# Another hand-searched step order for an attention-and-FFN kernel, up to its fifth chunk

## The chip, the cores and the metric

One core of one Trainium2 chip. The metric is the device time of one execution in microseconds (us). Engines are written as the profile writes them: PE (TensorE matmul), PEld (TensorE weight load, beside PE), DVE (VectorE), ACT (ScalarE), POOL (GpSimd), SP (SyncE, which here only issues DMAs; SPq is its sequencer).

## What is computed

A linear attention with a decaying state, and a squared-ReLU feed-forward network (FFN) on its output. Batch 4, 8 heads, 768 positions, head width 48, so 3072 tokens of width 384; the FFN is 2048 wide. All float32.

```python
for t in range(S):                                    # 768 positions
    kt, vt, rt, wt = (k[:, :, t], v[:, :, t], r[:, :, t], w[:, :, t])
    cur = np.einsum('bhd,bhe->bhde', u[None] * kt, vt)
    y[:, :, t] = np.einsum('bhd,bhde->bhe', rt, state + cur)
    state = wt[:, :, :, None] * state + np.einsum('bhd,bhe->bhde', kt, vt)
...
h = np.maximum(x @ w_in, 0.0)                         # x: y as 3072 x 384; w_in 384 x 2048
return (h * h @ w_out)                                # w_out 2048 x 384
```

## The kernel before

**Tiling.** The positions are cut into 6 chunks of 128; with 4 batches there are 24 attention units, "chunk c, batch b". The attention of a chunk makes x (the FFN's input, transposed); the FFN of the same chunk follows while the attention of the next chunk goes on between its steps. The FFN of a chunk runs over 16 blocks of 128 hidden columns. Every product is made of three matmuls, of a high and a low part of either factor. In chunk 1 and for the first blocks of chunk 0 a block is done in two halves, of two batches (256 columns of tokens) each; elsewhere all four batches together (512 columns). An FFN block has a position number x, counted in full blocks along the program: chunk 0 has x = 0 to 15 and so on. Its steps are:

- **hp at x** (L860): 9 matmuls into one of only two PSUM tiles `hp0`, `hp1`.
- **g1** (ACT, L865): ReLU into a tile t. **g2** (ACT L867 in chunk 0, DVE L869 after): the square, back into hp. **g3** (ACT, L871): the high part g. **g4** (DVE, L872): the low part, hp minus g. Only after g4 is the hp tile free again.
- **ob at x** (L878): 3 matmuls for each batch into its output tile `ob`. They need both parts of g, so g4 too.

**Attention steps that the prediction names.** On DVE: z0, z1 (L480, transposes of loaded rows of a pair of batches), scan (L535, four running sums a unit), rt, kn, kn2, kq (L552, L558, L559, L562, whole-tile products), S (L697, L812) and S2 (L700), mask (L709), xl (L614). On ACT: far, far2 (L604, L605), Ec (L557), exp (L543), ly (L801), rc2 (L521). On POOL from chunk 2 on: rk and ru (L584, L586). On PE: turn (L518), ktp (L635) and mix (L668 to L687 are one group for a unit). On SP: load (L471), v (L504), pt (L490) and the sends (L725), which copy pieces of x between partitions.

**Splitting the weights.** Each of 16 weight tiles is widened on ACT (L428), treated in three DVE steps (L432, L436, L441), rounded on ACT (L448) and its rest formed on POOL (L449).

**Order.** The kernel records 2446 steps in a `Plan` and then emits them by three tables of numbers: `ORDER` holds the step numbers in the order of emission, `PLACES` says which buffer of its pool each tile gets, and `FILLS` puts so many dummy 128x128 transposes (L351) on PE ahead of a step. Each engine works through its own steps in that order and waits, in order, for what a step needs.

```python
order, places, fills = self.table or (range(len(self.steps)), (), {})
...
for n in order:
    s = self.steps[n]
    assert all(d.n in done for d in s.deps), ("too early", n, s.name)
    ...
    place = pool[places[self.slots[k]]] if places else next(...)
    ...
    if n in fills:
        s.fill = fills[n]
```

Of the kernel before, what the change touches and what calls it, by code (L numbers as in the profile page):

```python
# [96 lines left out]
class Names:  # L97
# [18 lines left out]
    4, 14, 17, 19, 6, 16, 0, 5, 20, 1, 18, 26, 15, 11, 7, 23, 24, 25, 55, 58, 309, 21, 22, 27, 28, 8, 2, 13, 30, 9, 57, 31, 312, 59, 33, 56, 64, 10, 29, 61,  # L116
    32, 92, 12, 36, 60, 308, 65, 53, 93, 62, 67, 38, 52, 71, 37, 310, 39, 51, 66, 63, 72, 3, 68, 311, 40, 102, 69, 106, 70, 74, 94, 105, 41, 73, 103, 107, 75,
    77, 108, 43, 42, 44, 46, 54, 45, 47, 48, 76, 314, 327, 78, 95, 104, 79, 49, 315, 109, 50, 313, 80, 81, 96, 111, 316, 317, 112, 34, 35, 82, 143, 318, 113,
    326, 146, 83, 346, 329, 97, 330, 118, 328, 84, 319, 85, 86, 320, 149, 87, 88, 89, 114, 110, 119, 180, 148, 345, 344, 147, 321, 150, 347, 90, 322, 115,
    323, 459, 116, 460, 348, 466, 91, 461, 462, 100, 101, 467, 99, 98, 184, 145, 468, 142, 324, 117, 144, 152, 463, 331, 469, 190, 470, 153, 155, 332, 181,  # L120
    333, 198, 139, 325, 124, 334, 140, 159, 141, 121, 151, 126, 464, 154, 120, 465, 472, 335, 349, 122, 125, 160, 350, 127, 182, 161, 351, 352, 156, 183, 353,
    128, 223, 336, 195, 162, 224, 129, 131, 185, 196, 337, 130, 471, 133, 132, 217, 473, 197, 157, 365, 338, 135, 134, 136, 474, 363, 158, 339, 382, 475, 137,
    138, 340, 480, 354, 476, 481, 482, 355, 483, 477, 165, 166, 364, 163, 362, 191, 192, 356, 167, 366, 168, 484, 341, 342, 169, 357, 487, 385, 384, 214, 216,
    358, 359, 488, 494, 489, 490, 491, 123, 360, 170, 193, 383, 343, 479, 194, 478, 172, 171, 361, 173, 380, 175, 210, 225, 174, 486, 201, 226, 493, 495, 176,
    202, 485, 233, 281, 496, 381, 497, 367, 498, 177, 368, 501, 164, 239, 199, 492, 502, 240, 503, 504, 500, 508, 392, 369, 370, 509, 510, 221, 511, 371, 505,
    372, 515, 499, 516, 393, 398, 507, 394, 512, 506, 517, 395, 222, 513, 227, 518, 519, 373, 396, 211, 230, 188, 514, 229, 397, 246, 386, 228, 522, 523, 387,
    529, 520, 521, 524, 525, 526, 388, 207, 400, 401, 200, 419, 530, 248, 231, 402, 234, 531, 532, 374, 533, 208, 527, 375, 528, 232, 251, 242, 536, 537, 389,
    538, 539, 203, 204, 543, 390, 249, 540, 376, 399, 544, 178, 220, 403, 420, 243, 437, 189, 535, 377, 534, 545, 546, 547, 215, 250, 247, 205, 391, 378, 179,
    438, 404, 405, 406, 552, 553, 554, 542, 555, 218, 379, 556, 561, 410, 407, 541, 562, 551, 563, 206, 564, 416, 565, 548, 550, 187, 557, 256, 408, 276, 262,
    261, 209, 264, 560, 549, 263, 411, 412, 413, 235, 570, 212, 219, 418, 236, 559, 213, 569, 571, 414, 284, 292, 186, 283, 291, 290, 558, 289, 417, 439, 409,  # L130
    265, 452, 572, 573, 574, 568, 579, 436, 237, 422, 241, 259, 423, 567, 576, 580, 566, 260, 581, 238, 424, 458, 425, 578, 582, 280, 244, 426, 415, 245, 304,
    435, 453, 427, 575, 583, 421, 428, 457, 454, 456, 455, 257, 287, 434, 641, 258, 285, 253, 266, 429, 297, 430, 431, 288, 440, 709, 441, 286, 432, 267, 442,
    277, 295, 588, 589, 577, 269, 597, 590, 586, 584, 707, 268, 433, 708, 591, 305, 598, 599, 600, 592, 643, 270, 644, 587, 254, 446, 642, 301, 652, 595, 255,
    271, 443, 585, 302, 601, 273, 272, 447, 594, 650, 606, 448, 303, 444, 445, 649, 648, 654, 647, 274, 658, 656, 653, 278, 655, 660, 593, 602, 646, 607, 659,
    608, 603, 279, 710, 645, 740, 275, 711, 596, 651, 252, 657, 609, 449, 296, 293, 294, 298, 615, 661, 718, 610, 664, 282, 1007, 616, 604, 667, 612, 673,
    611, 617, 670, 618, 741, 1022, 713, 722, 605, 668, 715, 669, 675, 676, 674, 624, 684, 1023, 1024, 299, 671, 723, 450, 677, 686, 625, 614, 613, 680, 619,
    300, 626, 672, 683, 451, 621, 678, 663, 665, 622, 306, 627, 681, 685, 307, 623, 679, 682, 666, 620, 628, 687, 742, 635, 743, 744, 695, 698, 632, 775, 776,
    714, 717, 745, 777, 638, 694, 720, 782, 629, 700, 778, 783, 712, 724, 779, 719, 789, 1025, 630, 633, 690, 784, 780, 781, 701, 705, 697, 785, 786, 726,
    790, 704, 796, 721, 716, 634, 788, 693, 791, 792, 797, 732, 793, 787, 794, 746, 689, 1014, 798, 696, 799, 730, 1026, 1012, 800, 631, 731, 803, 729, 688,
    736, 810, 699, 795, 692, 802, 804, 1008, 1013, 1051, 805, 801, 1011, 806, 702, 807, 811, 812, 813, 814, 817, 1010, 703, 733, 818, 735, 734, 819, 820, 809,  # L140
    691, 737, 1053, 808, 706, 816, 824, 821, 1027, 725, 815, 1018, 738, 739, 1028, 822, 825, 826, 1009, 827, 831, 832, 828, 747, 823, 830, 1052, 748, 1017,
    1055, 728, 833, 834, 1054, 1015, 727, 749, 760, 758, 835, 1066, 755, 764, 756, 838, 839, 840, 845, 829, 837, 836, 841, 842, 846, 1068, 847, 1062, 1058,
    1065, 852, 848, 849, 1016, 757, 763, 761, 853, 854, 844, 762, 636, 1057, 859, 843, 855, 1059, 765, 851, 1061, 1063, 856, 1134, 1135, 1136, 1137, 860, 861,
    862, 1084, 1064, 850, 866, 857, 1019, 858, 1020, 639, 867, 1067, 1060, 863, 771, 868, 1021, 869, 865, 870, 873, 880, 1056, 767, 773, 1138, 1073, 874,
    1085, 770, 864, 871, 1076, 875, 772, 662, 876, 1075, 881, 872, 774, 769, 877, 878, 882, 879, 1074, 1123, 1139, 883, 752, 1080, 1029, 884, 759, 768, 891,
    754, 1069, 885, 1071, 1164, 751, 753, 1077, 1030, 766, 1078, 1086, 1087, 898, 892, 893, 894, 1124, 1079, 899, 637, 1081, 1031, 1088, 1039, 895, 1082,
    1083, 1040, 888, 750, 905, 889, 900, 901, 902, 1034, 1163, 1165, 896, 1038, 1037, 1046, 912, 640, 906, 1140, 1089, 897, 907, 1126, 908, 1044, 913, 1119,
    904, 1070, 1120, 1041, 1045, 909, 1090, 1033, 1091, 1048, 914, 911, 1092, 1050, 903, 1049, 1043, 1036, 1125, 1072, 919, 1035, 915, 1042, 1166, 1047, 1093,
    916, 926, 1032, 1167, 1121, 920, 921, 1104, 1122, 1196, 1127, 1103, 1128, 1101, 922, 1180, 1096, 1178, 1179, 1177, 910, 917, 1197, 1100, 1106, 1102, 1169,
    927, 1098, 923, 1108, 933, 1198, 1095, 1099, 1112, 1105, 928, 929, 1107, 1199, 1130, 1170, 918, 925, 930, 1174, 934, 924, 1398, 1399, 935, 936, 1097, 940,  # L150
    931, 937, 941, 942, 1110, 947, 1094, 1109, 1129, 932, 939, 943, 944, 1168, 1176, 954, 1200, 938, 1173, 1175, 1171, 1172, 948, 1115, 1181, 1131, 1132, 945,
# [867 lines left out]
```

## Time and profile before

| | |
|---|---|
| runs | 522.84, 522.40, 522.19 us; median 522.4 us |
| profiled execution, its time | 521.4 us |
| its span | 519.7 us |
| granted TensorE clock | 1.00 |
| PE busy | 506.6 us, 97% |
| PEld busy | 458.5 us, 88% |
| DVE busy | 358.3 us, 69% |
| ACT busy | 319.1 us, 61% |
| POOL busy | 87.8 us, 17% |
| DMA | 48.74 MB, mean 94 GB/s |

The span is the time between the first and the last recorded instruction; the execution's own time lies 1.7 us above it. Busy shares are means over the whole program: DVE and ACT are full in the first 54 us, where the weights are split, and far from full at the end. Idle time stands in the rows below in brackets, with the instruction that ended it.

### The profile page before, as it was taken

Reading aid. Unit: us, or ns where it says so; the run is one execution under the profiler, and the core shown is the slowest. Engines: PE = TensorE matmul, PEld = TensorE weight load, DVE = VectorE, ACT = ScalarE, POOL = GpSimd, SP = SyncE. Lnnn points to the kernel's source line nnn. Section 1 sums busy time; section 2 is a strip of 40 time slices with the busy share of each in tenths; the row PEclk is TensorE's granted clock in tenths of the full one; section 3 lists DMA queues with packets and bytes.
Section 4 is the critical chain, followed back from the end, with each engine's and each line's share of the span. In section 5 each row is a group of like instructions: output and inputs, shape, how many; then the busy total and the mean of one; then the engine's idle time right before and its main releaser. Section 6 shows DMA issues by size and latency. Waiting matters only on the chain.

```text
span 519.7 us, 13752 instructions
## 1 busy us (share of the span) xinstructions
PE 506.6 (97%) x5452; PEld 458.5 (88%) x5452; DVE 358.3 (69%) x787; ACT 319.1 (61%) x878; POOL 87.8 (17%) x133
## 2 busy tenths in 40 slices
PE   8999999999999999999998999999999999999996
PEld 7888898888999998899987989889988888998895
DVE  6999789898687988768778658678476354333332
ACT  4999898996766867666573656564543363433232
POOL 3025233344021040212203001303000000000000
PEclk9999999999999999999999999999999999999999
DMA  7999977363847765575772480661181000100001
GB/s 152 225 165 247 246 151 205 88 92 63 148 71 100 147 97 95 106 125 73 117 129 37 84 137 15 112 122 36 32 133 32 3 19 6 59 16 0 1 2 65
DMA packets 188310, 48.74 MB, mean 94 GB/s; under 512 B 178000, under 2 KB 183120, under 8 KB 188240
## 3 DMA queue, kind: packets, MB, share of 16 engines
q1 hardware_dynamic: 187520, 46.82, 47.6%
q8 instruction: 45, 0.74, 0.6%
q10 hardware_dynamic: 720, 0.98, 0.5%
q14 instruction: 25, 0.20, 0.1%
HBM read 31.65 MB, written 4.72 MB: 70 GB/s over the span
## 4 chain that ended last, share of the span: by engine, by line
PE 78%; SPq 5%; issue 5%; DVE 4%; ACT 4%; DMA 2%; POOL 1%; POOLq 0%; ACTq 0%; DVEq 0%
PE ob L878 35%; PE hp L860 34%; PE ob L668 2%; SPq L504 2%; PE ob L687 2%; DMA ri<-in_moe_w_in_dram 2%; PE a L677 2%; SPq L415 1%; PE a L650 1%; PE hp L635 1%; SPq L471 1%; POOL wi L449 1%; DVE pt L535 1%; ACT t L865 1%; DVE m L550 1%
## 5 line engine op out<-in xcount | busy, mean ns | idle before, releaser
L878 PE MATMUL ob<-wo,g 128*128 128x384 f32 x1152 | 227.0, 340 | 0.1
L860 PE MATMUL hp<-x,wi 128*128 128x512 f32 (+1 forms) x1062 | 221.8, 355 | 3.2 <-DVE g L872 2.5
L878 PEld LDWEIGHTS ob<-wo,g 128*128 128x128 f32 x1152 | 199.4, 188 | 8.1 <-DVE g L872 0.9
L860 PEld LDWEIGHTS hp<-x,wi 128*128 128x128 f32 x1062 | 174.1, 188 | 29.7 <-DVE g L872 3.7
L869 DVE SCALAR_TENSOR_TENSOR hp<-hp,t 128x512 f32<-128x512 f32 (+1 forms) x96 | 58.2, 606 | 74.5 <-ACT t L865 74.2
L865 ACT ACTIVATE t<-hp 128x512 f32<-128x512 f32 (+1 forms) x118 | 61.0, 517 | 72.2 <-PE hp L860 47.7
L872 DVE TENSOR_TENSOR g<-hp,g 128x512 fp32r<-128x512 f32 (+1 forms) x118 | 69.1, 587 | 35.5 <-ACT g L871 35.0
L871 ACT CAST g<-hp 128x512 fp32r<-128x512 f32 (+1 forms) x118 | 59.6, 506 | 49.5 <-DVE hp L869 48.6
L630 ACT ACTIVATE m<-diag,beta 128x64 f32<-128x64 f32 x160 | 40.4, 338 | 3.4 <-DVE beta L593 3.3
L658 POOL MEMSET S<- 1x1 f32 x20 | 2.2, 110 | 237.4 <-PE ob L668 237.4
L614 DVE SCALAR_TENSOR_TENSOR x<-ob,x 112x128 fp32r<-112x128 f32 x80 | 21.2, 284 | 19.3 <-ACT x L611 16.5
L822 ACT COPY ob<-zero 112x128 f32<-112x128 f32 x80 | 20.7, 270 | 17.3 <-PE ob L878 10.1
L611 ACT ACTIVATE x<-ob 112x128 fp32r<-112x128 f32 x80 | 19.1, 275 | 17.3 <-PE ob L687 12.1
L535 DVE TENSOR_TENSOR_SCAN pt<-pt,zero 112x128 f32<-112x128 f32 x64 | 27.2, 456 | 2.4 <-DMA x<-x 1.1
L449 POOL TENSOR_TENSOR wi<-q,wi 128x768 fp32r<-128x768 f32 x8 | 17.1, 2135 | 55.1 <-ACT wi L448 44.0
L584 POOL TENSOR_TENSOR st<-st 128x384 f32<-128x384 f32 x16 | 16.7, 1043 | 33.0 <-DVE st L480 32.5
L480 DVE STREAM_TRANSPOSE st<-st 128x1152 f32<-128x1152 f32 x16 | 21.6, 1363 | 0.0
L542 ACT ACTIVATE m<-pt 112x512 f32<-112x512 f32 x24 | 15.1, 631 | 9.2 <-DVE pt L535 8.2
L449 POOL TENSOR_TENSOR wo<-q,wo 128x768 fp32r<-128x768 f32 x8 | 15.9, 1983 | 18.1 <-ACT wo L448 14.8
L558 DVE TENSOR_TENSOR pt<-pt,m 112x512 f32<-112x512 f32 x24 | 16.9, 706 | 2.4 <-ACT Ec L557 1.3
L559 DVE SCALAR_TENSOR_TENSOR m<-pt,m 112x512 f32<-112x512 f32 x24 | 18.0, 748 | 0.3
L709 DVE COPY_PREDICATED m<-caus,a 128x256 f32<-128x256 uint8 x40 | 17.3, 439 | 0.9 <-PE a L650 0.9
(125 smaller groups left out, 540.0 us busy)
## 6 DMA issues: line engine op xcount, KB each, us to landing
pt<-st SPq DMA_DIRECT2D x96, 96.0 KB, 2.9
ro<-in_moe_w_out_dram SPq DMA_DIRECT2D x8, 768.0 KB, 6.1
v<-in_v_dram SPq DMA_DIRECT2D x96, 48.0 KB, 2.8
out_dram<-q SPq DMA_DIRECT2D x20, 192.0 KB, 2.1
ri<-in_moe_w_in_dram SPq DMA_DIRECT2D x32, 96.0 KB, 4.9
ri<-in_moe_w_in_dram SPq DMA_DIRECT2D x8, 384.0 KB, 6.1
st<-in_r_dram SPq DMA_DIRECT2D x8, 384.0 KB, 5.3
st<-in_w_dram SPq DMA_DIRECT2D x8, 384.0 KB, 4.9
```

Of the source, the lines that this page charges most:

```text
L449: P.add("pool", 1.9, rank(8 * k + 5), lambda q=q, tt=tt: G.tensor_tensor(out=tt[:, 1], in0=q.tile, in1=tt[:, 0].bitcast(F32), op=ALU.subtr ...
L480: V.transpose(out=zt[:, i].rearrange("a t p q i -> a t (p q) i"), in_=sv[:, :, i].rearrange("s t p q x -> s t (p q) x"))
L535: lambda p=p: V.tensor_tensor_scan(out=pt[:, 0, p], data0=src(0)[:, p], data1=zero.broadcast_to([HP, C]), initial=1.0, op0=ALU.mult, op1=A ...
L614: made.append(P.add("dve", c2, rank(nm + "l"), lambda y=y, hi=hi, lo=lo: V.scalar_tensor_tensor(out=lo(), in0=y(), scalar=-1.0, in1=hi().b ...
L630: A.activation(M.tile[:, o:o + Q], diag2, AF.Copy, scale=beta.tile[:, i:i + 1])
L822: P.add("act", 0.16, rank("zero"), lambda p=p: A.copy(out=obs[p][0:HP, DM:], in_=zero[0:HP].broadcast_to([HP, C])), w=[("YO", p)], after=t ...
L860: T.matmul(hp.tile[:, 0:n], wi[f][:, wl, kt], xT[:, kt, xl, xs], start=(m == 0), stop=(m == 3 * KT - 1))
L865: P.add("act", 0.49 if full else 0.28, rank("g1"), lambda: A.activation(t(), h(), AF.Relu), r=[hp], w=[(g, 1)])
L869: P.add("dve", 0.605 if full else 0.337, rank("g2"), lambda: V.scalar_tensor_tensor(out=h(), in0=h(), scalar=0.0, in1=t(), op0=ALU.max, op ...
L871: P.add("act", 0.48 if full else 0.26, rank("g3"), lambda: A.copy(out=hi(), in_=h()), r=[hp], w=[(g, 0)])
L872: P.add("dve", 0.605 if full else 0.335, rank("g4"), lambda: V.tensor_tensor(out=lo(), in0=h(), in1=hi().bitcast(F32), op=ALU.subtract), r ...
L878: T.matmul(obs[b][:, 0:DM], g.tile[0][:, gl, o:o + C], wo[f][:, wl], start=(f == 0 and m == 0), stop=(f == NF - 1 and m == 2))
```

## The change

Only the three tables differ. Every step, its instructions and its shapes are the same. From `zero of chunk 4, batch 0`, the 1739th of the 2446 steps, to the end the two orders are equal; before it nearly every engine's order differs in places. `FILLS` has 59 dummy transposes in place of 52.

```diff
 ORDER = (
-    4, 14, 17, 19, 6, 16, 0, 5, 20, 1, 18, 26, 15, 11, 7, 23, 24, 25, 55, 58, 309, 21, 22, 27, 28, 8, 2, 13, 30, 9, 57, 31, 312, 59, 33, 56, 64, 10, 29, 61,
...
 FILLS = {
-    16: (2, 'ob', 1), 55: (6, 'ob', 3), 30: (3, 'ob', 1), 57: (4, 'ob', 1), 71: (2, 'ob', 0), 48: (5, 'ob', 1), 82: (3, 'ob', 3), 89: (5, 'ob', 1),
-    145: (3, 'ob', 0), 144: (7, 'ob', 0), 127: (8, 'side', 0), 168: (4, 'side', 0),
+    16: (2, 'ob', 1), 15: (3, 'ob', 2), 57: (3, 'ob', 1), 55: (3, 'ob', 1), 71: (2, 'ob', 1), 41: (4, 'ob', 1), 77: (2, 'ob', 1), 80: (5, 'ob', 3),
+    143: (2, 'ob', 3), 459: (10, 'ob', 1), 145: (3, 'ob', 0), 144: (7, 'ob', 0), 127: (8, 'side', 0), 223: (3, 'side', 0), 473: (2, 'side', 0),
 }
```

What the tables do is seen in the order of the instructions. Three places follow; names end in a buffer number, and a row's last entry is its shape.

**DVE, around 74 to 79 us, the splits of weights 3 and 4 and the attention of chunk 1.** The last row is g4 at 12, the first full block (512 columns), which frees the tile for hp at 16. Before:

```order
L872 TENSOR_TENSOR g1_97<-hp0_151,g1_97 128x256
L432 TENSOR_SCALAR q1_156<-q1_156 128x768
L441 SCALAR_TENSOR_TENSOR q0_155<-ri4_72,q0_155 128x768
L558 TENSOR_TENSOR pt0_135<-pt0_135,m2_164 112x512
L872 TENSOR_TENSOR g2_99<-hp0_151,g2_99 128x256
L436 SCALAR_TENSOR_TENSOR q1_156<-ro3_70,q1_156 128x768
L812 TENSOR_TENSOR S3_140<-a1_154,Ec3_172 112x96
L441 SCALAR_TENSOR_TENSOR q1_156<-ro3_70,q1_156 128x768
L872 TENSOR_TENSOR g0_95<-hp1_152,g0_95 128x512
```

The same stretch of the changed kernel:

```order
L872 TENSOR_TENSOR g1_97<-hp1_152,g1_97 128x256
L432 TENSOR_SCALAR q1_156<-q1_156 128x768
L441 SCALAR_TENSOR_TENSOR q0_155<-ri4_72,q0_155 128x768
L436 SCALAR_TENSOR_TENSOR q1_156<-ro3_70,q1_156 128x768
L872 TENSOR_TENSOR g2_99<-hp0_151,g2_99 128x256
L441 SCALAR_TENSOR_TENSOR q1_156<-ro3_70,q1_156 128x768
L552 TENSOR_TENSOR pt0_135<-pt0_135 112x4x127
L558 TENSOR_TENSOR pt0_135<-pt0_135,m3_165 112x512
L559 SCALAR_TENSOR_TENSOR m3_165<-pt0_135,m3_165 112x512
L872 TENSOR_TENSOR g0_95<-hp1_152,g0_95 128x512
```

L436 of weight 3 (q1) now follows directly on L441 of weight 4 (q0); rt, kn and kn2 (L552, L558, L559) stand between L441 of weight 3 and g4.

**DVE, around 276 to 282 us, where chunk 4's attention begins.** L480 are z0 and z1 of batches 2 and 3, L535 the scans of batch 1, and the first L872 of each piece is g4 at 88. Before:

```order
L535 SCALAR_TENSOR_TENSOR pt0_135<-pt0_135,zero_126 112x128
L614 SCALAR_TENSOR_TENSOR x1_141<-ob2_149,x1_141 112x128
L480 STREAM_TRANSPOSE st0_157<-st1_158 128x1152
L869 SCALAR_TENSOR_TENSOR hp1_152<-hp1_152,t0_96 128x512
L480 STREAM_TRANSPOSE st0_157<-st1_158 128x1152
L535 SCALAR_TENSOR_TENSOR pt0_135<-pt0_135,zero_126 112x128 x3
L872 TENSOR_TENSOR g0_95<-hp1_152,g0_95 128x512
```

The same stretch of the changed kernel:

```order
L535 SCALAR_TENSOR_TENSOR pt0_135<-pt0_135,zero_126 112x128
L480 STREAM_TRANSPOSE st0_157<-st1_158 128x1152 x2
L614 SCALAR_TENSOR_TENSOR x1_141<-ob2_149,x1_141 112x128
L872 TENSOR_TENSOR g0_95<-hp1_152,g0_95 128x512
L697 TENSOR_TENSOR S10_173<-a0_153,S0_137 112x96
L535 SCALAR_TENSOR_TENSOR pt0_135<-pt0_135,zero_126 112x128
```

Three scans between z1 and g4 at 88 are moved behind it: one soon after, the other two after g4 at 92 and after g2 at 94. On PE, the first step that needs g4 at 88 was hp at 92, right behind hp at 90; now three ob at 88 stand between the two.

**SP, around 208 to 216 us, where chunk 2's x is completed.** L725 are the sends of its last batch; L889 is a store of an output. Before:

```order
L504 DMA v2_161<-in_v_dram 64x4x48 x2
L471 DMA st1_158<-in_w_dram 128x16x48
L889 DMA out_0_dram<-q1_156 128x384
L504 DMA v0_159<-in_v_dram 64x4x48
L725 DMA x0_142<-x3_168 16x2x256 x6
```

The changed kernel:

```order
L504 DMA v2_161<-in_v_dram 64x4x48
L504 DMA v0_159<-in_v_dram 64x4x48 x2
L471 DMA st1_158<-in_r_dram 128x16x48
L725 DMA x0_142<-x3_168 16x2x256 x6
L504 DMA v0_159<-in_v_dram 64x4x48
```

The six sends move ahead of that store, of a load (`in_w_dram`) and of a v.

## Rows read from the trace of the kernel before

**Rows 1.** The page: busy times of the engines, and the chain that ended last.

```profile
PE 506.6 (97%) x5452; PEld 458.5 (88%) x5452; DVE 358.3 (69%) x787; ACT 319.1 (61%) x878; POOL 87.8 (17%) x133
PE 78%; SPq 5%; issue 5%; DVE 4%; ACT 4%; DMA 2%; POOL 1%; POOLq 0%; ACTq 0%; DVEq 0%
```

**Rows 2.** Busy times by window: stretch, length, busy time (instructions), PEclk, DMA share, GB/s.

```profile
16.00:54.00 38.00, 35.50 (x515) 31.42 (x512) 35.43 (x67) 34.56 (x95) 11.05 (x6) 1.00 0.94 213
54.00:300.00 246.00, 242.82 (x2910) 222.25 (x2909) 199.25 (x444) 178.73 (x515) 59.47 (x76) 1.00 0.62 113
300.00:515.00 215.00, 214.67 (x1906) 192.72 (x1904) 112.18 (x235) 97.47 (x245) 13.15 (x31) 1.00 0.24 45
```

**Rows 3.** The waits of PE: what waited for what, total, times, longest.

```profile
PE hp L860 <- DVE g L872: 2.5, 2, 1.5
PE hp L518 <- DVE g L872: 0.9, 1, 0.9
```

**Rows 4.** Timeline near 50 us: start, length, engine and instruction, idle before it.

```profile
48.84 0.84 ACT L448 CAST wo<-q 128x768 fp32r<-128x768 f32 x1
49.46 0.96 DVE L436 SCALAR_TENSOR_TENSOR q<-ro,q 128x768 uint32<-128x768 uint32 x1
...
49.75 2.36 POOL L449 TENSOR_TENSOR wo<-q,wo 128x768 fp32r<-128x768 f32 x1 [2.11 <-ACT wo L448]
...
50.46 2.47 DVE L441 SCALAR_TENSOR_TENSOR q<-ro,q 128x768 uint32<-128x768 uint32 x1
...
53.31 0.65 PE L518 MATMUL hp<-ident,st 128*112 128x128 f32 x4 [0.87 <-DVE g L872]
```

**Rows 5.** Timeline from 74 to 80 us.

```profile
74.00 0.69 DVE L558 TENSOR_TENSOR pt<-pt,m 112x512 f32<-112x512 f32 x1 [1.29 <-ACT Ec L557]
...
74.78 1.84 POOL L449 TENSOR_TENSOR wi<-q,wi 128x768 fp32r<-128x768 f32 x1 [6.75 <-ACT wi L448]
74.94 2.49 DVE L436 SCALAR_TENSOR_TENSOR q<-ro,q 128x768 uint32<-128x768 uint32 x1
...
79.13 1.44 PE L860 MATMUL hp<-x,wi 128*128 128x512 f32 x5 [0.96 <-DVE g L872]
```

**Rows 6.** Timeline from 276 to 282 us.

```profile
277.85 1.00 POOL L584 TENSOR_TENSOR st<-st 128x384 f32<-128x384 f32 x1
277.88 3.42 DVE L535 TENSOR_TENSOR_SCAN pt<-pt,zero 112x128 f32<-112x128 f32 x3
278.05 2.37 PE L860 MATMUL hp<-x,wi 128*128 128x512 f32 x9
...
281.22 0.66 DVE L872 TENSOR_TENSOR g<-hp,g 128x512 fp32r<-128x512 f32 x1
...
281.94 2.36 PE L860 MATMUL hp<-x,wi 128*128 128x512 f32 x9 [1.52 <-DVE g L872]
```

**Rows 7.** Two lines of DVE over the whole program: minimum, median, maximum ns.

```profile
L441 DVE SCALAR_TENSOR_TENSOR q<-ro,q x8: 943/954/2468, 29.4 to 117.0; 128x768 uint32<-128x768 uint32 x8
...
L535 DVE TENSOR_TENSOR_SCAN pt<-pt,zero x64: 398/414/1251, 137.5 to 401.5; 112x128 f32<-112x128 f32 x64
```

**Rows 8.** Timeline around 200 us.

```profile
199.66 1.71 PEld L878 LDWEIGHTS ob<-wo,g 128*128 128x128 f32 x10 [0.38 <-DVE g L872]
...
201.96 0.60 PE L635 MATMUL hp<-ident,pt 112*128 112x112 f32 x4 [0.27 <-DVE pt L562]
```

**Rows 9.** Timeline from 208 to 217 us.

```profile
208.63 1.64 SPq L889 DMA_DIRECT2D out_dram<-q  x1
...
211.03 4.27 SPq L725 DMA_DIRECT2D x<-x  x6
...
214.53 2.63 DVE L480 STREAM_TRANSPOSE st<-st 128x1152 f32<-128x1152 f32 x2
...
216.82 3.52 PE L860 MATMUL hp<-x,wi 128*128 128x512 f32 x14 [0.31 <-DMA x<-x]
```

**Rows 10.** Timeline near 31 us: the fills in front of a waiting step.

```profile
31.66 0.93 PE L351 MATMUL ob<-ident 128*128 128x128 f32 x7
```

201 rows, old and new, of tables (ORDER, PLACES) are left out of this document.

## Prediction

> **What bounds the kernel now.** The page comes first. PE is busy 506.6 of 519.7 us and holds 78% of the chain that ended last [rows 1]; the clock is 1.00 all through, so it costs nothing that an order could give back. An order can only remove waits of PE, so the next view is busy time by window [rows 2]. From 300 us on, the part whose order stays, PE is idle 215.00 - 214.67 = 0.33 us. From 54 to 300 us it is idle 246.00 - 242.82 = 3.18 us, and from 16 to 54 us 38.00 - 35.50 = 2.50 us. In that second stretch PE is not the pace: DVE (35.43 of 38) and ACT (34.56) are nearly gapless and the DMA share is 0.94, while PE's own gaps are partly stuffed with dummy transposes, which count as busy: seven of them take 0.93 us, 0.13 each [rows 10].
>
> So what the change can remove as visible idle time is 2.50 + 3.18 = 5.7 us. The waits list says where most of it lies: three waits, 2.5 + 0.9 = 3.4 us, are all for a g4 [rows 3]. The timelines then show why each g4 was late, and it is one pattern three times. A DVE step with two operands in SBUF runs beside a POOL step and takes far longer than elsewhere: L441 2.47 us beside a POOL L449 [rows 4], with 0.954 as its median [rows 7]; L436 2.49 beside an L449 [rows 5]; three scans in 3.42 beside L584 [rows 6], with 0.414 each as the median [rows 7]. In each case the DVE step ends when the POOL step does, plus its own normal length: L449 ends at 49.75 + 2.36 = 52.11, L441 at 52.93. The g4 queued right behind it is late, and PE, which needs the hp tile that g4 frees, waits 0.87, 0.96 and 1.52 us.
>
> **The change, part by part.** No instruction of work is added or removed, so PE's work costs the same; seven fills more cost 7 x 0.13 = 0.9 us at the very most, and nothing where they stand in a wait. All else is a question of which wait goes and which comes.
>
> *The scans at 278 us.* Before, hp at 92 stands directly behind hp at 90 on PE, so g4 at 88 has only the 2.37 us of hp at 90 as cover, and it stands behind three held scans (3.42 us) [rows 6]. After, these scans stand behind g4, and on PE three ob at 88, which need g4 too, stand between hp at 90 and hp at 92; g4 loses 3.42 us of predecessors against a wait of 1.52. The two scans held back to g4 at 92 and g2 at 94 then meet the POOL steps, or miss them, with nothing of PE right behind. I take the whole wait: **-1.5** (bounds 0 and -1.5). What is late next is rt of that unit, and with it its mix, which PE needs only several FFN blocks later.
>
> *hp at 16, 79 us.* L436 of weight 3 now follows on L441 of weight 4 without kn and a half-size g4 between, so it is issued about a microsecond sooner and should start before the POOL step that held it; also the 1.29 us in which DVE waited for Ec [rows 5] goes, as kn is behind the splits. Against that rt, kn and kn2, some 0.69 each [rows 5], now stand ahead of g4 at 12, and two of these were not there before. Removed 2.49 - 0.95 = 1.5 and 1.3, added 2 x 0.69 = 1.4, and the following L441 may be held by the same L449 for up to its 1.84 us. The net, 1.4 without the last and -0.4 with it, is on average about half of the wait of 0.96: **-0.5** (bounds -1.0 and +0.4).
>
> *The first half of the FFN, 50 us.* On ACT the L448 that lets POOL start (48.84, 0.84 us [rows 4]) stands behind two more ACT steps after the change (rc2, a whole-tile step, for which I put the 0.69 of one [rows 5], and ly, a small one; together 0.9, an estimate), so L449 would start near 50.6 in place of 49.75; L441 would start at 50.46 plus whatever DVE is late by then (one step of xl and some scans are moved ahead, which I put at a quarter to one microsecond). If L441 starts first it takes 0.95 and the wait of 0.87 is gone; if L449 does, L441 ends at 50.6 + 1.84 + 0.95 = 53.4, half a microsecond later than the 52.93 of before. These two are nearly even. I take **-0.3** (bounds -0.9 and +0.6).
>
> *The waits near 200 us.* PEld waits 0.38 for a g4 and PE 0.27 for kq [rows 8]. More ob steps stand between hp and the first of them afterwards; I take that one whole and nothing of the other: **-0.4** (bounds 0 and -0.65).
>
> *The sends of chunk 2.* They are issued from 211.03 to 215.30, and hp at 64 waits 0.31 for the last to land [rows 9]. After the change they stand in front of a store whose issue took 1.64 us and of a load and a v, so the last lands earlier by more than 0.31: **-0.3** (bounds 0 and -0.3). Loads and v of a later chunk go that much later; a v is needed by mix, many blocks on.
>
> *New waits.* The moves also shorten covers. In front of g4 at 40, z1 and z0 now stand back to back, 2.63 us for two as in [rows 9], where one z and a mask stood, while what PE has between hp at 40 and hp at 42 gets no longer; in front of g4 at 78 a rt of 0.69 is put; z1 of chunk 4's first pair stands behind a later load. Each of these has little or no slack, and each costs nothing if DVE comes there with none of its work late. The nearest rows for one that fails are the three waits of before, 0.87 to 1.52. I take one of 0.9 and 0.1 for fills: **+1.0** (bounds 0 and +3.0, two or three failing at once).
>
> [...] The row shows L441 ending 0.82 us behind the L449 beside it [rows 4], about its own normal length: nothing of it went on meanwhile. [...]
>
> *Sum:* -1.5 - 0.5 - 0.3 - 0.4 - 0.3 + 1.0 = **-2.0 us**. The profiled execution took 521.4, so it would take 519.4. It lies 1.0 below the median of the runs, 522.4; moved by the same, the median of the changed kernel is **520.4 us**. Its own range, from one new wait more to none and the even case at 50 us won, is 519.0 to 521.6.
>
> **The rivals.**
>
> *More goes than named.* No new wait, the L441 at 50 us free, and the head of the FFN quicker because PE's stuffed gaps before 54 us shrink too: 520.4 - 1.0 - 0.6 - about 1 (less than the 2.50 idle in that window [rows 2]) gives 517.8. For it: DVE and ACT are so full up to 54 us that a better order there counts in full. Against it: the DMA share of 0.94 in the same stretch, which no order lowers.
>
> *The waits only change place.* POOL's 59.47 us between 54 and 300 us and DVE's 199.25 [rows 2] are the same steps; they must meet somewhere as often as before. The new places at x = 40 and 78 and at 50 us cost what the old ones did: 522.4, within 1.0. For it: the old order hid all but three or four meetings as well. Against it: at 278 us PE gets cover that it did not have, whatever POOL does.
>
> *Slower.* VectorE steps are held by POOL just ahead of a g4 in new places. At 1.1 us each (the mean of 0.87, 0.96 and 1.52), with the 1.5 at 278 us gained, it decides from the third such wait on: four give -1.5 - 0.7 + 4 x 1.1 = +2.2, or 524.6. For it: covers at 40 and 78 are short, and the even case at 50 us. Against it: many half-block covers of chunk 1 grew.
>
> **How the numbers follow.** The sum's own case 0.46; more goes 0.13; waits change place 0.23; slower 0.18. A measurement of this kernel can tell about 0.2%, 1.0 us. Faster by more (under 521.4): 0.13 of more goes and 0.44 of the sum's own, 0.57. Within: 0.21 of the places changed and 0.02 of the sum's own, 0.23. Slower: 0.18 and 0.02, 0.20. The range of 517.4 to 523.6 leaves out about 0.04 below and 0.14 above.
>
> **What would show it.** Right: in the profile after, the waits of PE for g4 in the waits list fall from 3.4 us to about 1.5; PE near 278 us has no bracket; idle time from 54 to 300 us falls from 3.2 to near 1.5; L441 near 50 us takes 0.95. Wrong: a new bracket `<-DVE g L872` on PE of a microsecond or more at hp at 42, hp at 82 or in chunk 3's blocks; the turn of chunk 1's first batch later than 53.31; or PE working through from 300 us on at another length than the 215 us of before, since nothing there is moved.

## The result and the profile after

The changed kernel takes 527.1 us (median of 9 runs, 523.6 to 528.7) against 522.4 before (521.1 to 522.8): a ratio of 1.0089, 95% interval 1.0064 to 1.0114. It is slower by 4.7 us where 2.0 less was forecast. Its runs spread over 5.1 us, those of before over 1.7. Ratios leave out an execution that lies over 1.5% above the fastest of its kernel; there was one, in poolgap.

The profiled execution took 528.71, the longest of the nine; its span is 526.7. The page's busy times, its chain that ended last and its row of the granted clock (40 slices, tenths):

```profile
PE 510.6 (97%) x5459; PEld 462.6 (88%) x5459; DVE 363.1 (69%) x787; ACT 320.0 (61%) x878; POOL 86.8 (16%) x133
PEclk9979999999899999999999999999999999999998
PE 79%; DVE 5%; issue 5%; SPq 4%; ACT 3%; DMA 2%; POOL 1%; DVEq 0%; POOLq 0%; ACTq 0%
```

PE is busy 4.0 us longer [rows 1], and seven more dummy transposes of 0.13 us each [rows 10] are at most 0.9 of it; some of the rest is work at a lower clock, which fell in two places (to 0.50 from 26 to 32 us and from 132 to 134 us). The waits of PE:

```profile
PE hp L860 <- DVE g L872: 2.3, 2, 2.1
PE ob L518 <- DMA st<-in_w_dram: 2.2, 2, 1.8
...
PE ob L878 <- DVE x L614: 1.5, 1, 1.5
PE hp L518 <- DVE g L872: 1.0, 1, 1.0
```

Of the list of before [rows 3] the 1.52 us at 282 us is gone; there is a longer wait for g4, one for a load and one for xl (L614). Busy times by window (PE first, the clock third from the end) put the loss ahead of 200 us:

```profile
16.00:54.00 38.00, 36.11 (x475) 32.10 (x475) 31.84 (x62) 31.34 (x86) 8.38 (x4) 0.91 0.89 200
54.00:100.00 46.00, 42.93 (x369) 38.94 (x367) 41.96 (x60) 41.07 (x100) 17.45 (x9) 1.00 0.94 208
100.00:200.00 100.00, 98.13 (x1315) 92.10 (x1314) 81.92 (x197) 73.55 (x224) 26.79 (x37) 0.98 0.50 85
200.00:300.00 100.00, 99.95 (x1246) 90.65 (x1245) 78.66 (x185) 61.95 (x186) 17.96 (x32) 1.00 0.55 96
```

From 200 to 300 us PE is now idle 0.05 us.

**The start.** The turn of chunk 0, batch 3 waits 1.76 us for a load that SP issued at 20.12 (18.84 in before), and the clock falls behind that wait. Timeline:

```profile
20.12 0.42 SPq L471 DMA_DIRECT2D st<-in_w_dram  x1
...
24.27 0.65 PE L518 MATMUL ob<-ident,st 128*112 128x128 f32 x4 [1.76 <-DMA st<-in_w_dram]
```

Windows of 2 us from 22 to 34 us:

```profile
22.00:24.00 2.00, 0.50 (x7) 0.20 (x2) 1.97 (x5) 1.18 (x4) 0.00 (x0) 1.00 1.04 229
24.00:26.00 2.00, 1.73 (x14) 1.65 (x14) 1.64 (x5) 0.80 (x3) 1.73 (x1) 0.88 1.06 314
26.00:28.00 2.00, 2.00 (x28) 1.69 (x26) 0.32 (x2) 0.21 (x1) 0.26 (x1) 0.50 0.53 119
...
30.00:32.00 2.00, 2.00 (x12) 2.00 (x11) 1.18 (x3) 1.79 (x5) 0.00 (x0) 0.50 1.10 221
32.00:34.00 2.00, 2.00 (x17) 2.00 (x16) 1.38 (x2) 0.77 (x2) 0.00 (x0) 0.91 1.04 223
```

PE worked 0.50 of 2 us and then stood at a granted clock of 0.50 from 26 to 32 us, back at 1.00 from 33 us on. VectorE and ScalarE wait for it there: they are busy 0.32 and 0.21 us from 26 to 28, ScalarE idle 2.99 us for PE (L780), VectorE 2.54 for ScalarE behind that.

**hp at 16.** Where half a microsecond was to be gained, POOL's two L449 hold rt and kn2, which the change had put in front of g4 at 12. Timeline:

```profile
78.45 2.07 POOL L449 TENSOR_TENSOR wi<-q,wi 128x768 fp32r<-128x768 f32 x1 [4.83 <-ACT wi L448]
78.73 2.34 DVE L552 TENSOR_TENSOR pt<-pt 112x508 f32<-112x508 f32 x1
...
81.11 2.38 POOL L449 TENSOR_TENSOR wo<-q,wo 128x768 fp32r<-128x768 f32 x1 [0.58 <-ACT wo L448]
...
81.83 2.20 DVE L559 SCALAR_TENSOR_TENSOR m<-pt,m 112x512 f32<-112x512 f32 x1
...
83.96 0.68 DVE L872 TENSOR_TENSOR g<-hp,g 128x512 fp32r<-128x512 f32 x1
...
84.69 1.20 PE L860 MATMUL hp<-x,wi 128*128 128x512 f32 x4 [2.09 <-DVE g L872]
```

L436 was freed as forecast (0.95 us for 2.49 [rows 5]); the steps behind it took its place, and the wait grew from 0.96 [rows 5] to 2.09.

**130 us, not named in the prediction.** kn of chunk 1, batch 3 is held through rk's end, an L449 and two ru (L586) that follow one another on POOL without a gap. Behind it stand mask, S and xl; xl frees the tile that a zero (L822) must clear before the next ob. Timeline:

```profile
124.68 4.53 DVE L558 TENSOR_TENSOR pt<-pt,m 112x512 f32<-112x512 f32 x1
124.89 1.83 POOL L449 TENSOR_TENSOR wo<-q,wo 128x768 fp32r<-128x768 f32 x1
...
126.69 1.97 POOL L586 TENSOR_TENSOR st<-st,un 128x384 f32<-128x384 f32 x2
128.61 0.94 POOL L492 MEMSET pt<- 16x1024 f32 x1
...
129.97 3.72 PE L878 MATMUL ob<-wo,g 128*128 128x384 f32 x12 [1.55 <-DVE x L614]
```

kn ends at 129.21, 0.55 us behind the last ru (128.66).

**The scans.** Here the forecast held: g4 at 88 is done at 286.72, long before hp at 92, which has no bracket [rows 6]. Timeline:

```profile
285.48 2.37 PE L860 MATMUL hp<-x,wi 128*128 128x512 f32 x9
286.04 0.68 DVE L872 TENSOR_TENSOR g<-hp,g 128x512 fp32r<-128x512 f32 x1
...
286.80 0.85 DVE L535 TENSOR_TENSOR_SCAN pt<-pt,zero 112x128 f32<-112x128 f32 x1
...
289.57 2.73 PE L860 MATMUL hp<-x,wi 128*128 128x512 f32 x11
```

**PE's lag.** To compare orders, I let a profile's PE steps run through in order of their start, weigh each with the figure that the plan records with it (2.085 for a full hp, no fills), and ask when the same sum is reached. Lag is that time less the time in the profile of before; a positive lag means later than before. The figures are only a ruler. The kernels after the second column are the experiments below; "fall" marks a stretch in which the granted clock was under 1.00.

```
time in before   50.2   71.8   83.1  115.0  136.3  192.8  225.3  271.1  288.2  513.4
after            3.71f  3.93   5.02   4.85   8.55f  8.16   6.79   6.95   5.48   5.36
after2           1.76f  1.99   3.03   3.03   6.97f  6.55   5.18   5.38   3.91   3.75
fill143         -0.05   0.19   1.25   1.08   4.48   4.40   3.75   3.90   2.45   2.31
hp16             0.34   0.54   0.40   0.95   4.48   4.65   3.28   3.45   2.00   1.92
kn298           -0.26   0.05   2.62f  2.26   3.72   3.29   1.92   2.07   0.59   0.44
poolgap          0.16   0.38   1.44   1.25   3.78   3.36   2.00   2.14   0.69   0.59
fix3             0.56   0.80   0.67   0.49   1.94   1.51   1.08   1.20  -0.25  -0.35
nofill           4.22f  4.20   4.20   4.26   4.26   4.43   3.23   3.56   3.57   3.56
b276a           -0.72  -0.72  -0.69  -0.67  -0.67  -0.67  -0.07  -0.08  -1.82  -1.95
(f: fall of the clock in the stretch that ends here)
```

Two rows show how far the lag moves without a change of order: nofill has the order of before throughout, b276a up to 276 us. b276a moves by 0.7 ahead of 50 us, and between 192.8 and 225.3 us one rises by 0.6 and the other falls by 1.2. Elsewhere, with before's order and no fall of the clock, they move by 0.35 at most. A smaller difference in those two stretches says nothing of an order.

### The profile page after: what moved, and what is told of

It reads as the page before. It is cut to its first block, busy times and chain, and to the rows that moved or that the text cites. A ratio compares the mean times of both kernels' runs of the same rounds, so it can differ in the third digit from the quotient of the medians.

```text
span 526.7 us, 13763 instructions
## 1 busy us (share of the span) xinstructions
PE 510.6 (97%) x5459; PEld 462.6 (88%) x5459; DVE 363.1 (69%) x787; ACT 320.0 (61%) x878; POOL 86.8 (16%) x133
## 4 chain that ended last, share of the span: by engine, by line
PE 79%; DVE 5%; issue 5%; SPq 4%; ACT 3%; DMA 2%; POOL 1%; DVEq 0%; POOLq 0%; ACTq 0%
PE ob L878 36%; PE hp L860 34%; PE ob L668 2%; PE ob L687 2%; PE a L677 2%; PE a L650 1%; PE hp L635 1%; SPq L504 1%; DMA ro<-in_moe_w_out_dram 1%; SPq L415 1%; DMA v<-in_v_dram 1%; SPq L471 1%; DVE pt L558 1%; DVE g L872 1%; ACT q L428 1%
## 5 line engine op out<-in xcount | busy, mean ns | idle before, releaser
L872 DVE TENSOR_TENSOR g<-hp,g 128x512 fp32r<-128x512 f32 (+1 forms) x118 | 69.1, 587 | 43.1 <-ACT g L871 42.6
L614 DVE SCALAR_TENSOR_TENSOR x<-ob,x 112x128 fp32r<-112x128 f32 x80 | 20.6, 283 | 20.3 <-ACT x L611 15.7
L822 ACT COPY ob<-zero 112x128 f32<-112x128 f32 x80 | 20.8, 268 | 22.1 <-DVE x L614 16.3
L449 POOL TENSOR_TENSOR wi<-q,wi 128x768 fp32r<-128x768 f32 x8 | 16.0, 1999 | 62.1 <-DMA st<-in_w_dram 20.7
L535 DVE TENSOR_TENSOR_SCAN pt<-pt,zero 112x128 f32<-112x128 f32 x64 | 25.5, 433 | 0.4 <-DMA v<-in_v_dram 0.3
L480 DVE STREAM_TRANSPOSE st<-st 128x1152 f32<-128x1152 f32 x16 | 21.4, 1356 | 0.2 <-ACT st L605 0.2
L558 DVE TENSOR_TENSOR pt<-pt,m 112x512 f32<-112x512 f32 x24 | 20.3, 845 | 1.4 <-ACT m L543 1.0
L584 POOL TENSOR_TENSOR st<-st 128x384 f32<-128x384 f32 x16 | 17.2, 1078 | 21.6 <-DVE st L480 10.9
L449 POOL TENSOR_TENSOR wo<-q,wo 128x768 fp32r<-128x768 f32 x8 | 15.9, 1989 | 22.4 <-ACT wo L448 18.8
L559 DVE SCALAR_TENSOR_TENSOR m<-pt,m 112x512 f32<-112x512 f32 x24 | 19.3, 805 | 0.4
L552 DVE TENSOR_TENSOR pt<-pt 112x508 f32<-112x508 f32 x24 | 19.0, 791 | 0.2
```

The lines of the kernel that those rows point to most:

```text
L449: P.add("pool", 1.9, rank(8 * k + 5), lambda q=q, tt=tt: G.tensor_tensor(out=tt[:, 1], in0=q.tile, in1=tt[:, 0].bitcast(F32), op=ALU.subtr ...
L480: V.transpose(out=zt[:, i].rearrange("a t p q i -> a t (p q) i"), in_=sv[:, :, i].rearrange("s t p q x -> s t (p q) x"))
L535: lambda p=p: V.tensor_tensor_scan(out=pt[:, 0, p], data0=src(0)[:, p], data1=zero.broadcast_to([HP, C]), initial=1.0, op0=ALU.mult, op1=A ...
L558: P.add("dve", 0.6, rank("kn"), lambda: V.tensor_tensor(out=pt[:, 0], in0=pt[:, 0], in1=yv(), op=ALU.mult), r=[y0], w=EK, port=True)
L822: P.add("act", 0.16, rank("zero"), lambda p=p: A.copy(out=obs[p][0:HP, DM:], in_=zero[0:HP].broadcast_to([HP, C])), w=[("YO", p)], after=t ...
L872: P.add("dve", 0.605 if full else 0.335, rank("g4"), lambda: V.tensor_tensor(out=lo(), in0=h(), in1=hi().bitcast(F32), op=ALU.subtract), r ...
```

## The experiments

`PLACES` goes with each order: a tile keeps the buffer of the table that its step comes from, or takes the free one where that is taken. Where an order is cut together from two, `FILLS` is that of the kernel whose steps come first. Ratios are against runs of the kernel before on the same chip, with 95% intervals.

**Which part of the order.**

```diff
+ORDER = before[:290] + [n for n in after if n not in before[:290]]      # b55a
+ORDER = after[:275] + [n for n in before if n not in after[:275]]       # a55b
```

b55a. 

> The order of before for its first 290 steps (to about 55 us), then the steps that are left in the order of after. If the loss lies in the start (theory: at 22 us PE waits 1.76 us for a late load, and its granted clock then stands at half for 8 us), the clock is 1.00 up to 55 us and the time is about 523.5: 527.1 less some 4, with the later waits near 83 and 128 us still there. Rival (the loss lies in the waits for VectorE at 83 and 128 us): 526 to 527.

a55b. 

> The order of after for its first 275 steps (to about 55 us), then the order of before. Theory (loss in the start): 525.5 to 527, with the clock below 1.00 near 26 to 34 us. Rival (loss in the later waits): within 0.5 of 522.4.

b55a took 526.0 (ratio 1.0070, 1.0042 to 1.0098), a55b 523.4 (1.0027, 1.0002 to 1.0053). So the start makes about 1 us of the loss and the rest nearly all: the rival of b55a, while a55b lies between its theory and its rival. The 4 us of lag that the one profile of after shows at the start are not the usual case.

**The wait at 22 us.**

```diff
 FILLS = {
-    143: (2, 'ob', 3),
+    143: (18, 'ob', 3),
```

fill143. 

> After, with 18 dummy transposes in place of 2 ahead of the turn that waits for the late load at 22 us: 2.1 us more of dummy work on PE inside a wait of about 2. Theory (what costs is mostly the halved clock that follows the idle stretch): the clock stays at 1.00 from 20 to 40 us, and the time falls by 2 to 3, to about 524.5. Rival (the start is paced by loads, VectorE and ScalarE, and the clock costs nothing there): 527 to 527.5.

```diff
 ORDER = (                   # 95: the load; 52, 54, 53, 51: the v pieces
-    312, 52, 72,
+    312, 95, 52, 72,
...
-    103, 95, 111,
+    103, 111,
```

load95. 

> After, with one load (the in_w rows of chunk 0, batch 3) issued on SP ahead of the four v pieces that stood in front of it, about 3 us earlier. Theory (the late load causes the wait and, through it, the halved clock): no wait for in_w at 22 us, clock 1.00 there, 523 to 524. Rival (the start as a whole is slower in the new order, and the next late thing takes the wait's place): 526 to 527.

fill143 took 526.6 (1.0091, 1.0060 to 1.0122), load95 527.3 (1.0087, 1.0054 to 1.0119). In fill143's profile the clock stays at 1.00 and the lag at 50 us is -0.05, so at that place the theory holds; but its other five runs have clocks of 0.985 to 0.995, and the median does not move. In load95's profile the wait for in_w at 22 us is gone, but PE waits 1.14 us for a v at 39 us and the clock falls at 12 to 16 us instead, with no wait of PE above 0.43 us in front of the fall: the rival.

**The two places on VectorE.**

```diff
 ORDER = (                   # hp16: 202, 204, 205 are rt, kn, kn2; 547 is g4 at 12
-    535, 202, 204, 378, 232, 205, 547,
+    535, 378, 232, 547, 202, 204, 205,
```

hp16. 

> After, with rt, kn and kn2 of chunk 1, batch 0 moved on VectorE from in front of g4 at 12 to right behind it. Theory (of the 2.09 us that PE waits at hp at 16, all is what POOL's two L449 add to rt, 2.34 us, and kn2, 2.20 us, of 0.69 each): the wait is gone or under 0.5, no clock fall follows near 84 us, and the time falls by 1.1 to 2 to about 525.5. Rival (the held steps only move on, to the weight splits behind them, and the wait comes back a few blocks later): within 0.7 of 527.1.

```diff
 ORDER = (                   # kn298: 298, 299 are kn, kn2; 674 is the third xl
-    1022, 298, 713,
+    1022, 713,
...
-    642, 299, 624, 674,
+    642, 624, 674, 298, 299,
```

kn298. 

> After, with kn and kn2 of chunk 1, batch 3 moved on VectorE behind the third xl of batch 1, so that the kn that took 4.53 us beside four POOL steps in a row no longer stands in front of mask, S and xl. Theory (that kn makes the 1.55 us of PE at 130 us and what follows, 3.4 us of PE's lag between 115 and 136 us in the profiles so far): PE has no wait for L614, the lag in that stretch falls to 1 or less, time 524 to 525. Rival (ktp of that unit, which needs kn, takes the wait over, or the lag there has another cause): within 1 of 527.1.

fix3 is both moves and fill143's fills. 

> After, with the two moves on VectorE of the two runs before it and 18 dummy transposes ahead of the turn at 22 us. Theory (three separate costs that add, and three gains at 200, 215 and 278 us worth 2 to 2.8 together): 520 to 521.5, under before, with the clock near 1.00. Rival (a common cause, such as VectorE as a whole being late): 524 to 526.

hp16 took 524.9 (1.0060, 1.0035 to 1.0085), near the theory, though its interval overlaps that of the changed kernel. hp at 16 has no bracket any more, and the lag between 71.8 and 83.1 us of before falls from +1.1 to -0.1; part of it comes back as a wait of 0.98 at a turn, behind a kn that now takes 2.23. Its profile also carries the wait at 22 us, with no fall behind it:

```profile
24.06 0.65 PE L518 MATMUL ob<-ident,st 128*112 128x128 f32 x4 [1.88 <-DMA st<-in_w_dram]
```

The window behind it:

```profile
24.00:28.00 4.00, 3.94 (x51) 3.73 (x52) 2.05 (x7) 1.94 (x9) 2.00 (x1) 1.00 0.87 206
```

The same order with the same wait lags 0.34 there without the fall and 3.71 with it.

kn298 took 523.9 (1.0028, 1.0008 to 1.0049), the time that the theory said. No wait for L614 is left; the lag from 115 to 136 us grows by 1.5 in place of 3.7 (3.4 without a fall, in fill143), not by 1 or less. What remains is a wait of 1.3 for g4 at ktp of that unit, the one that the rival named:

```profile
124.29 2.29 DVE L558 TENSOR_TENSOR pt<-pt,m 112x512 f32<-112x512 f32 x1
...
128.50 0.67 DVE L872 TENSOR_TENSOR g<-hp,g 128x512 fp32r<-128x512 f32 x1
...
129.23 0.60 PE L635 MATMUL hp<-ident,pt 112*128 112x112 f32 x4 [1.31 <-DVE g L872]
```

fix3 took 522.7 (1.0020, 1.0001 to 1.0039), between theory and rival. So the three places together make about 3.6 us of the loss (1.0089 to 1.0020). Its profile, at clock 1.00 and the second fastest of its twelve runs, ends 0.35 ahead of before. The costs add nearly as assumed, less the 1.3 that stays at ktp.

**What holds kn.**

```diff
 ORDER = (                   # poolgap: 1023, 741 are ru, the others its readers; 662 is SE
-    451, 684, 1023, 1024, 1025, 683, ..., 741, 742, 685, ..., 712, 662, 303, ..., 743,
+    451, 684, 683, ..., 685, ..., 712, 662, 1023, 741, 1024, 1025, 742, 743, 303, ...,
```

poolgap. 

> After, with two ru steps of chunk 2 moved on POOL behind the SE of chunk 1, batch 1, so that rk, L449, ru, ru no longer follow one another without a gap beside kn of chunk 1, batch 3. Theory (kn is held for as long as POOL goes from one step to the next without a gap): kn takes 2.7 us or less in place of 4.53, the wait of PE for L614 near 130 us falls from 1.55 to under 0.3, the time by about 1.5 to 525.5. Rival (kn is held by one step and its length has another cause): kn over 4 us, 527.

It took 525.5 (1.0079, 1.0047 to 1.0111; its runs go from 522.3 to 527.6, with one of 531.4; without that one the median is 524.5). The interval holds the ratio of the changed kernel, so its time decides nothing; its profile does. kn takes 2.57, and PE has no wait for L614. But the ru steps, moved, now hold kn2, and PE waits at ktp instead:

```profile
121.08 2.57 DVE L558 TENSOR_TENSOR pt<-pt,m 112x512 f32<-112x512 f32 x1
121.26 1.84 POOL L449 TENSOR_TENSOR wo<-q,wo 128x768 fp32r<-128x768 f32 x1
...
124.43 1.98 POOL L586 TENSOR_TENSOR st<-st,un 128x384 f32<-128x384 f32 x2
124.47 2.49 DVE L559 SCALAR_TENSOR_TENSOR m<-pt,m 112x512 f32<-112x512 f32 x1
...
128.74 0.60 PE L635 MATMUL hp<-ident,pt 112*128 112x112 f32 x4 [1.63 <-DVE g L872]
```

So kn's length here follows the row of POOL steps beside it: 4.53 us with four in a row, 2.57 with two. It is no rule that a held step waits for the whole row. In the profile of the changed kernel, at 70 us, rt gets in behind the first of two L449 without a gap, and the second L449 is the one held:

```profile
69.54 1.84 POOL L449 TENSOR_TENSOR wi<-q,wi 128x768 fp32r<-128x768 f32 x1 [8.31 <-DMA ri<-in_moe_w_in_dram]
70.50 1.43 DVE L552 TENSOR_TENSOR pt<-pt 112x508 f32<-112x508 f32 x1
71.34 2.28 POOL L449 TENSOR_TENSOR wo<-q,wo 128x768 fp32r<-128x768 f32 x1
```

In the profile of before the very kn of this unit gets in between a ru and a rk:

```profile
119.10 1.00 POOL L586 TENSOR_TENSOR st<-st,un 128x384 f32<-128x384 f32 x1
119.43 1.22 DVE L558 TENSOR_TENSOR pt<-pt,m 112x512 f32<-112x512 f32 x1 [0.85 <-ACT m L543]
120.07 1.46 POOL L584 TENSOR_TENSOR st<-st 128x384 f32<-128x384 f32 x1
```

rt ends at 71.93 and kn at 120.65, each 0.55 us behind the POOL step that held it, as the long kn does behind its last ru. Why a held step gets in behind one POOL step and not behind another no run shows.

**The clock.**

```diff
 FILLS = {                   # fillall: 561 is hp at 16, 605 the ob that waits at 130 us
+    143: (18, 'ob', 3), 561: (15, 'free', 0), 605: (11, 'free', 1),
...
 FILLS = {                   # nofill: the kernel before, its 52 fills taken out
-    16: (2, 'ob', 1), 55: (6, 'ob', 3), 30: (3, 'ob', 1), 57: (4, 'ob', 1), 71: (2, 'ob', 0), 48: (5, 'ob', 1), 82: (3, 'ob', 3), 89: (5, 'ob', 1),
-    145: (3, 'ob', 0), 144: (7, 'ob', 0), 127: (8, 'side', 0), 168: (4, 'side', 0),
```

fillall. 

> After, with dummy transposes in all three of its long waits: 18 in place of 2 at 22 us, 15 ahead of hp at 16, 11 ahead of the ob at 24 that waits at 130 us. The waits stay as they are; only PE is not idle in them. Theory (half of the loss is the halved clock that comes after such idle stretches in some executions: mean clock 0.993 against 0.998, 0.005 x 522 = 2.6 us; the other half the waits themselves): mean clock 0.997 or more, 524 to 525. Rival (the clock falls for another reason than these waits): clock 0.993, 526 to 527.5.

nofill. 

> Before, without its 52 dummy transposes; the waits ahead of 54 us are the same, only that PE is idle in them. Theory (what PE does before a wait ends decides whether its clock falls, and the fall costs the new order half of its loss): the clock falls in the first 54 us in most executions, mean clock 0.990 to 0.995, 524 to 527. Rival (the fills do nothing but take their 0.13 us each; the clock falls for other reasons): 521.5 to 522.5 and a mean clock as that of before, 0.998.

after2 is the changed kernel itself. 

> The changed kernel once more, for a second profile. Theory (the waits are the program's, the clock falls are chance): the waits for g4 near 83 us and for L614 near 130 us, 2.1 and 1.5 us, stand again within 0.3, and the clock has fallen in other places than 26 to 34 and 131 to 135 us, or not at all. Rival (the clock falls belong to these two waits): the same two stretches at half clock.

nofill took 524.6 (1.0043, 1.0016 to 1.0070) with a mean clock of 0.989: the theory's time, and a clock just under its 0.990 to 0.995. The fall in its profile comes after a window in which PE worked 1.69 of 4 us:

```profile
8.00:12.00 4.00, 1.69 (x13) 1.37 (x12) 3.23 (x6) 2.75 (x9) 0.71 (x1) 1.00 0.98 181
12.00:26.00 14.00, 13.67 (x165) 12.25 (x166) 8.80 (x21) 9.63 (x32) 0.00 (x0) 0.54 0.99 223
```

fillall took 526.1 (1.0072, 1.0046 to 1.0097) with a mean clock of 0.997 where after has 0.993, yet not the time that was expected. Two of its six runs took 523.2 and 523.4 at 1.000, the others 525.8 to 528.2 at 0.989 to 0.998, more than their clocks explain (the line fitted below to runs of before gives 522.2 to 526.9 for them, an estimate). The third of its fills itself waited 1.35 us, for an S, so that place stayed open.

after2 took 525.6. Its waits stand again: 2.06 for g4, 1.69 for L614, 1.32 for the load. The clock fell behind the load and behind L614, as in the first profile, for a shorter time behind the load and as long behind L614 (mean clock of the execution 0.992 against 0.988): that is nearer to the rival. Over all profiles it is not fixed: behind the wait at 22 us it fell in after and after2 (1.76 and 1.32 us) and not in hp16 and poolgap (1.88 and 1.5); behind that at 83 us (2.06 to 2.28) in b55a, load95 and kn298, and not in after, after2, fill143 and poolgap; behind that for L614 (1.54 to 1.69) in after, after2 and b55a, and not in fill143, hp16 and load95.

**The gains, alone.**

```diff
+ORDER = before[:826] + [n for n in after if n not in before[:826]]      # b150a; 1137 in b200a, 1553 in b276a
```

b150a. 

> The order of before for its first 826 steps (to about 150 us), then what is left in the order of after. Theory (all of the loss lies ahead of 150 us, and the gains behind it are real: PE's lag falls by 2.0 to 2.8 us from 200 to 290 us in every profile of the new order so far): 522.4 less 2 to 2.8, about 520, with no wait of PE for g4 at 215 or 282 us. Rival (these gains are only time given back that was lost earlier, when VectorE has got ahead during the waits): 522 to 523.

b200a. 

> The order of before for its first 1137 steps (to about 200 us), then what is left in the order of after. Theory (the waits at 215 and 282 us go, as they did in every profile of the new order so far, and nothing takes their place; the wait of 1.03 us that the cut at 150 us made is not there): 2.0 under before, 520.0 to 520.5. Rival (the gain needs VectorE as it stands in the new order, ahead of its work; from the old order's stand the scans come late again): 521.5 to 522.4, with a wait near 282 us.

b276a. 

> The order of before for its first 1553 steps (to about 276 us), then what is left in the order of after: of the changes, only the spread scans and the ob steps around hp at 92. Theory (the term of the scans is right and stands alone): no wait of PE near 282 us, 1.5 under before, 520.5 to 520.9. Rival (the stretch has given its gain only where VectorE was ahead): a wait of PE near 280 us, 521.5 to 522.5.

b150a took 521.5 (0.9990, 0.9973 to 1.0007): no verdict, since the cut made a wait of 1.03 at 152 us, though its profile ends 2.3 ahead of before. b200a took 524.9 (1.0063, 1.0039 to 1.0087): its cut made PE wait 2.72 us at 202 us for a copy (L887), so it tells nothing of the sum; at 282 us it has no wait. b276a has a cut without a wait and took 520.7 (0.9973, 0.9950 to 0.9996): the theory, and a kernel faster than both. In its profile hp at 92 has no bracket:

```profile
277.80 0.38 DVE L535 TENSOR_TENSOR_SCAN pt<-pt,zero 112x128 f32<-112x128 f32 x1
...
279.04 0.68 DVE L872 TENSOR_TENSOR g<-hp,g 128x512 fp32r<-128x512 f32 x1
...
282.27 2.03 PE L860 MATMUL hp<-x,wi 128*128 128x512 f32 x8
```

## Why the prediction was wrong

The sum was -2.0 with a term of +1.0 for new waits; measured is +4.7. The profile of fill143, whose clock stays at 1.00 until its end, gives the terms without the clock; they add to +2.3. It is one execution, the fastest of its six: its span is 2.4 us longer than that of before, and that of fillall's profile, also at clock 1.00, 1.8.

- *The scans at 278 us*, -1.5: right. The lag falls by 1.45 in fill143, 1.47 in after, and b276a shows the gain alone. The prediction's reading that each DVE step ends with the POOL step beside it plus its own length was too simple here: the scans end at 281.30, 2.45 us behind the one L584 in [rows 6]. The trace has an L586 from 278.93 to 279.95 and a second L584 from 279.91 to 281.02 there, and the scans take 1.25, 1.17 and 1.15 us.
- *The waits near 200 us* and *the sends of chunk 2*, -0.4 and -0.3: right in sign, their size is not shown. The lag between 192.8 and 225.3 us falls by 0.65 in fill143 and 1.4 in after, but by 1.2 in nofill too, which has the order of before.
- *The first half of the FFN, 50 us*, -0.3: the even case fell to POOL. L449 started at 54.22 and L441 at 54.30, so L441 took 2.56 and the wait stayed at 0.98 for 0.87. No profile of the new start has it otherwise, so what an L441 that starts ahead of L449 would have gained there is not shown. This cost 0.1, within the bounds.
- *hp at 16, 79 us*, -0.5: **failed**, +1.1. The step at fault is "the following L441 may be held by the same L449": L441 passed, and two L449, not one, met rt and kn2, which I had priced at 0.69 each. They took 2.34 and 2.20, and hp16, in which these steps stand behind g4, has no wait there. The bound of +0.4 was worked out with one meeting.
- *New waits*, +1.0: **failed** in place and size. At x = 40 and 78 nothing waits. The lag grows by 3.4 between 115.0 and 136.3 us, past the bound of 3.0, where kn is held by four POOL steps in a row. With kn moved behind xl (kn298, fix3) it grows by 1.5, so 1.9 of the 3.4 goes with the place of the held kn; what makes the rest, with its wait of 1.3 for g4 at ktp, no run takes apart. I looked for g4 alone as the victim; here it is xl, and through zero the next ob.
- "The clock is 1.00 all through, so it costs nothing that an order could give back": **failed** as a step, since an order can also take it. In 33 runs of the kernel before, the time follows the mean clock along 521.1 us + 527 us x (1 - clock), a line fitted to them. Their mean clock is 0.998 and that of the nine runs of after 0.993: by this line 0.0049 x 527 = 2.6 us, an estimate. With the +2.3 of the waits that makes 4.9 against the 4.7 measured, but the split is not shown. The line does not carry over: nofill's mean clock of 0.9885 would make 527.2 us by it, and 524.6 was measured; and among the nine runs of after the time hardly follows the clock (the three at 0.997 took 526.1 to 528.4).

Of the signs set out beforehand, PE near 282 us without a bracket came. PE's waits for g4 stayed at 3.3 us, its idle time from 54 to 300 us rose to 4.99 (3.07 + 1.87 + 0.05), and L441 took 2.56; of the signs of being wrong, the turn came late, at 57.26. The rival that came true is the slower one: its own mechanism at one place in front of a g4 and at another in front of an xl, with the clock as a second cause that it lacked. That its +2.2 lies near fill143's +2.3 is luck, since it was worked out with four waits of 1.1 for g4. At 50 us L441 started 0.08 us behind L449 and ended 0.82 us behind its end, so it waited for the whole of that step, as in [rows 4]; at 125 us the trace shows more than that, since kn waited through three further POOL steps behind the rk beside which it began (an L584 that ends at 124.92), and by the wait for that one alone it would have taken under 1 us, an estimate: the 0.24 us to rk's end and its own 0.69.

Open is what makes one execution of the new order differ from the next by up to 5 us: falls of the clock may be a part (in poolgap 522.3 us came with a clock of 0.997, 527.6 with 0.991), but in after and poolgap runs whose mean clocks differ by at most 0.001 still differ by 2 to 5 us. Which waits vary there no run showed.

## What to carry to other kernels

When an order moves a step out of a meeting with another engine, look for what comes to stand in the place that it leaves: here DVE's 787 steps took 363.1 us in place of 358.3, POOL held the next two-operand steps (rt and kn2, 2.34 and 2.20 us where some 0.69 each was expected), and what counted was what stood behind that one. Count the steps that follow one another without a gap on the other engine, since a held step can wait for the whole row (kn: 4.53 us beside four, 2.57 beside two). And where the clock can fall behind an idle stretch, as PE's did to 0.50 behind the wait of 1.76 us, price a new one of a microsecond or two above its length: with nearly the same wait at 22 us (1.88 and 1.76) the lag at 50 us was 0.3 us or 3.7.

## What the runs showed of the hardware

- A VectorE step with two operands in SBUF (kn at 125 us in after) waited through four POOL steps in a row: 4.53 us in place of 0.69, and ended 0.55 us after the last that reads SBUF, beside a memset. With two POOL steps it took 2.57 (poolgap). Elsewhere such a step got in behind the first of two POOL steps without a gap (1.43 us at 70 us in after, 1.22 at 119 us in before), and the second POOL step was held (2.28 us in place of 1.84, and 1.46 in place of 1.00).
- TensorE's granted clock fell to 0.50 (26 to 32 us in after, 22 to 26 us in nofill), for 3 to 14 us at a time (131 to 135 us in after; 0.54 from 12 to 26 us in nofill). In after, after2, b55a, load95 and kn298 this came after waits of PE of 1.3 to 2.3 us, and in other profiles it did not with the same wait (1.76 us in after: a fall; 1.88 in hp16: none). In nofill it fell after 1.69 of 4 us of work, in load95 at 12 us with no wait above 0.43 in front.
- A fall costs more in one place than in another. Stretch times (1 - clock) is 3.4 us at 24 us in after, 1.7 at 83 us in kn298 and 1.7 at 131 us in after. The lag that came with it is 3.4 us at 24 us, where VectorE and ScalarE wait for PE (2.54 us, through ScalarE, and 2.99); 1.5 at 83 us (2.6 in kn298 against 1.1 in after); 0.3 at 131 us (3.7 in after against 3.4 in fill143). Why so little came of the last no run shows.
- The kernel before has runs with a mean clock under 1.000 as well: those at 0.994 to 0.997 take 521.8 to 525.5 us, those at 1.000 take 520.6 to 522.2.
